# Two matmul layers behind a linear recurrence: full 128-row passes for the last 64 features, and another engine for the scaling of the weights

## The chip, the cores and the metric

One core of a Trainium2 chip runs the whole program. The metric is the device time of one execution in microseconds (us); lower is better. The engines named below are TensorE (PE; its weight loads are listed apart as PEld), VectorE (DVE), ScalarE (ACT), GpSimd (POOL) and SyncE (SP), whose queue issues the DMAs.

## What is computed

The reference has three stages. The first is a recurrence over 768 steps for 4 x 8 heads of 40 features; its output is laid out as 3072 tokens of 320 features. The other two are layers with 2048 hidden units each:

```
x = attention(r, k, v, w, a, b)          # (3072, 320), float32
h = x @ w_in;   x = (h * cos(h)) @ w_out
h = x @ w_in2;  x = (s * relu(h)**2 + b) @ w_out2
```

The weights come as 64-bit floats. The answer has to be near that of float32, and the kernel reaches it with pairs of 16-bit numbers: a value is kept as a high half (rounded to 16 bits) and a low half (what the rounding left out), and a product is made of high x high, high x low and low x high.

## The kernel before, in words

The tokens are cut into 12 chunks of 256 (4 batches x 64 steps). For each chunk the program runs the recurrence (`prep`, `chain`), then layer one (`m1_*`), then layer two (`m2_*`). A layer's 2048 hidden units are 16 blocks `ff` of 128, taken in 8 pairs `p`. For one block TensorE makes the hidden values `hp` (128 hidden units by 256 tokens, `first`), ScalarE, VectorE and GpSimd turn them into two 16-bit halves `gh` and `gl` (`m1_g`, `m2_g`), and TensorE makes the output sums `op` out of these (`m1_s`, `m2_s`).

**The product with 320 features.** The contraction over 320 features is cut into 128 + 128 + 64 rows. The first two parts take three passes each: high weights x high input, high x low, low x high. The 64-row rest is packed. Its tile of weights has 128 rows: one half of the rows holds the high weights, the other half the low ones (`rows` says which half; it changes with every pair `p`), and the inputs are there twice, in the rows 0 to 63 and 64 to 127. One pass over all 128 rows with the high inputs gives high x high and low x high together. What is left is high weights x low inputs over 64 rows alone: this is the tail. `tail` issues it as a matmul with 64 rows, and `tails` brings two of them side by side, that of the last block of the pair before and that of the first block of this pair, since these lie in different halves of the rows. So a block has seven passes of 128 rows and a tail of 64 rows, each with 256 columns. A tail clears the accumulation of its `hp` tile (`start`) for the first block of a pair, and `hp` of pair p is complete only when `tails` of pair p + 1 has run; so `mlp` calls `m1_g` or `m2_g` of pair p behind the first block of pair p + 1.

**The weights.** Each block of weights is loaded as 64-bit words; three VectorE instructions turn these into float32 in place (`float32`). Then `w_in_chunk` and `w_out_chunk` make the halves: ScalarE writes the high half (times 1024), GpSimd multiplies the float32 block by 1024 in place, and GpSimd subtracts the high half from it, which gives the low half. For `w_in` the subtraction is two instructions: one over 128 rows and 256 columns, and one over the 64 rows of the packed part. For half of the blocks of the second layer's `w_out` (`k % 4 < 2`, 8 of 16) one VectorE instruction multiplies and subtracts, and GpSimd has nothing to do. The first layer's weights are made during the first chunk of the recurrence; those of the second layer are made when the buffers of the recurrence come free, near the end of it (12 blocks into the freed space, then 4 more).

**What sets the order.** The program is first recorded, instruction by instruction (`Recorder.add`), and a planner (`Recorder.schedule`) with its own costs for each instruction then gives every engine its order; `emit` (line 406) issues it, so that almost every row of the profile has line 406, and the tiles' names tell the rows apart. Work of layer one is so placed between the short matmuls of the recurrence. An engine runs its own list strictly in that order.

**Names.** `hp` are the hidden sums, `op` and `opx` the output sums, `xs` and `x2s` the inputs of layer one and two; `w`, `w2b`, `wraw` are blocks of `w_in`, `v`, `v2b`, `vraw` blocks of `w_out`; `kb`, `kbh`, `kbl` and `ar`, `arh`, `arl` are inputs of the recurrence with their halves, `XX` its decays, `yhl` its result. The lines of the text are: `w_in_chunk` 578, `w_out_chunk` 590, `tail` 1043, `tails` 1048, `first` 1055, `mlp` 1236.

Of the kernel before, what the change touches and what calls it, by code (L numbers as in the profile page):

```python
# [10 lines left out]
F32 = mybir.dt.float32  # L11
# [4 lines left out]
AF = mybir.ActivationFunctionType  # L16
ALU = mybir.AluOpType
# [9 lines left out]
NC = S // C  # L27
NFF = FF // 128
TB = B * C
# [3 lines left out]
SW = 1024.0  # L33
# [412 lines left out]
class Fast:  # L446
# [131 lines left out]
    def w_in_chunk(self, dst, name, k):  # L578
        nc = self.nc
        st = self.float32(self.RAW["i", dst.tensor.name, k])  # L580
        m = self.wtags[3] // 128
        wv = dst[:, k * m:k * m + m].rearrange("p f a n -> p a f n")
        sv = st.rearrange("p a (f n) -> p a f n", f=m)
        nc.scalar.activation(wv[:, 0:3], sv, AF.Copy, scale=SW)
        nc.gpsimd.tensor_scalar(out=st, in0=st, scalar1=SW, scalar2=1.0, op0=ALU.mult, op1=ALU.mult)
        nc.gpsimd.tensor_tensor(out=wv[:, 3:5], in0=sv[:, 0:2], in1=wv[:, 0:2], op=ALU.subtract)
        r = slice(64 - self.rows(k * m), 128 - self.rows(k * m))
        nc.gpsimd.tensor_tensor(out=wv[r, 2], in0=sv[r, 2], in1=wv[r, 2], op=ALU.subtract)

    def w_out_chunk(self, dst, name, k):  # L590
        nc = self.nc
        st = self.float32(self.RAW["o", dst.tensor.name, k])
        nc.scalar.activation(dst[:, k, 0], st, AF.Copy, scale=SW)
        if name == "v2" and k % 4 < 2:
            nc.vector.scalar_tensor_tensor(out=dst[:, k, 1], in0=st, scalar=SW, in1=dst[:, k, 0], op0=ALU.mult, op1=ALU.subtract)
            return
        nc.gpsimd.tensor_scalar(out=st, in0=st, scalar1=SW, scalar2=1.0, op0=ALU.mult, op1=ALU.mult)
        nc.gpsimd.tensor_tensor(out=dst[:, k, 1], in0=st, in1=dst[:, k, 0], op=ALU.subtract)

    def w_in_test(self, parts, name, k):  # L600
# [439 lines left out]
        for h in range(2):  # L1040
            self.nc.sync.dma_start(out=x[h * 64:h * 64 + 64, :, 2], in_=v[:, 256:320].rearrange("f p n -> p f n"))

    def tail(self, ps, w, x, ff):

        r = slice(self.rows(ff), self.rows(ff) + 64)
        self.nc.tensor.matmul(ps[:, ff % 2], w[ff][r, 2], x[r, 2, 1], start=(ff % 2 == 0), stop=True, skip_group_check=True)

    def tails(self, p, w, x):
        hp = self.HP
        hp[p] = self.ph.tile([128, 2, TB], F32, tag="at", bufs=8, name="hp")  # L1050
        if p:
            self.tail(hp[p - 1], w, x, 2 * p - 1)
        self.tail(hp[p], w, x, 2 * p)

    def first(self, p, k, w, x):
        ff, hp = 2 * p + k, self.HP
        for a, i, b in ((0, 0, 0), (0, 0, 1), (1, 1, 0), (1, 1, 1), (2, 2, 0), (3, 0, 0), (4, 1, 0)):
            self.nc.tensor.matmul(hp[p][:, k], w[ff][:, a], x[:, i, b], start=False, stop=True, skip_group_check=True)
        if ff == NFF - 1:
            self.tail(hp[p], w, x, ff)  # L1060


    def m1_t(self, c, p):
        x = self.XS[c]
        self.tails(p, self.W1, x.rearrange("p f i k t -> p i k f t"))

    def m1_f(self, c, p, k):
        x = self.XS[c]
# [32 lines left out]
    def x2(self, j):  # L1101
# [7 lines left out]
        for m in range(2):  # L1109
# [4 lines left out]
                for b in range(2):  # L1114
                    nc.tensor.transpose(ps[:, i, b], q[:, b, m, i * 128:i * 128 + 128], self.ident)
            nc.vector.tensor_copy(xs[:, :, :, m], ps)

    def m2_t(self, j, p):
        x = self.XS[NC + j]
        self.tails(p, self.W2, x.rearrange("p i b m t -> p i b (m t)"))  # L1120

    def m2_f(self, j, p, k):
        x = self.XS[NC + j]
# [109 lines left out]
                  (self.yt, c, pg), (self.ts, c, pg)]:  # L1233
            self.do(*f)

    def mlp(self, t, f, g, s, j, lo=0, hi=NFF // 2 + 2):
        lag = 2
        for p in range(lo, hi):
            for k in range(2):
                if p < NFF // 2:  # L1240
                    if k == 0:
                        self.do(t, j, p)
                    self.do(f, j, p, k)
                if k == 0 and 1 <= p <= NFF // 2:
                    self.do(g, j, p - 1)
                if p >= lag:
                    self.do(s, j, p - lag, k)
        if s == self.m1_s:
            self.nc.base[self.nc.blk] = (NC - 1 - j) * 22

    def run(self, es0):
        tc, nc = self.tc, self.nc
        for n in ("AN BT A0 UF M1 DT RAW HL UN UD X XV V TT G IN KB AR Z ND U RP R SS SD SHL XT M2 XS HP GH OP Y").split():
            setattr(self, n, {})
        with ExitStack() as es:
            pc = es0.enter_context(tc.tile_pool(name="const", bufs=1))
            dr = es.enter_context(tc.tile_pool(name="dram", bufs=1, space=DRAM))
            self.x0 = dr.tile([NC, 2, H, D, 4 * C], F16, name="x0")
            self.x1 = dr.tile([NC, 2, 128, DM], F32, name="x1")
            self.consts(pc)  # L1260
            rec = self.nc = Recorder(nc, {"any": {"at", "xs", "q"}, "cls": {"XT": 3, "rhp": 3, "hp": 3, "op": 2, "xs": 2, "M2": 2, "q": 4, "att": 6}})
            rec.sink.add(self.junk.tensor.name)
            pool = lambda s, n, **k: rec.pool(s.enter_context(tc.tile_pool(name=n, bufs=1, **k)), n)
            self.pm = pool(es, "mlp")
            self.ph = self.po = self.pp = pool(es, "psum", space=PSUM)
            pw = pool(es, "wt")
            self.w1 = pw.tile([128, NFF, 5, 128], F16, name="w1")
            self.v1 = pw.tile([128, NFF, 2, DM], F16, name="v1")
            es_p, es_a = ExitStack(), ExitStack()
            self.pst = pool(es_p, "prep", side="right")  # L1270
            self.pa = pool(es_a, "attn")
            self.XX = self.pa.tile([128, 4, 32, 33], F32, name="XX")
            self.ST = {pg: self.pa.tile([128, 8, 40], F32, name=f"ST{pg}") for pg in range(2)}
            self.YT = self.pst.tile([128, 16, 32], F32, name="YT")
            rec.vector.tensor_copy(self.YT[:, :, 16:32], bc(self.up[:, 0:16], 1, [128, 16, 16]))
            self.wtags = self.pm, "xs", 5, 128
            self.ff0 = 0
            self.W1, self.V1 = ([t[:, f] for f in range(NFF)] for t in (self.w1, self.v1))
            m1 = self.m1_t, self.m1_f, self.m1_g, self.m1_s
            m2 = self.m2_t, self.m2_f, self.m2_g, self.m2_s  # L1280
            self.prep(0)
            for c in range(NC):
                if c + 1 < NC:
                    self.prep(c + 1)
                if c == 0:
                    self.weights("w1", "v1", self.w1, self.v1)
                self.chain(c, 0)
                self.chain(c, 1)
                self.do(self.xs, c)
                self.do(self.x1_load, c)  # L1290
                if c < NC - 1:
                    self.mlp(*m1, c)
                else:
                    self.nc.base[self.nc.blk] = 26
                if c == 3:
                    self.tests("w1", "v1", (self.w1,), (self.v1,), 250)
            rec.schedule(until=("prep",))
            es_p.close()
            es_v = ExitStack()
            pv = pool(es_v, "late_v", side="right")  # L1300
            n = 12
            v2 = pv.tile([128, n, 2, DM], F16, name="v2")
            w2 = pv.tile([128, n, 5, 128], F16, name="w2")
            self.second(w2, v2, 0)
            self.W2, self.V2 = ([t[:, f] for f in range(n)] for t in (w2, v2))
            self.do(self.x2, 0)
            self.mlp(*m2, 0, 0, n // 2)
            half = dict(self.HP), dict(self.GH)
            self.mlp(*m1, NC - 1)
            self.HP, self.GH = half  # L1310
            rec.schedule(until=("attn",))
            es_a.close()
            es_b = ExitStack()
            self.pb = pool(es_b, "late")
            v2b = self.pb.tile([128, NFF - n, 2, DM], F16, name="v2b")
            w2b = self.pb.tile([128, NFF - n, 5, 128], F16, name="w2b")
            self.wtags = self.pb, "braw", 8, 128
            self.second(w2b, v2b, n)
            self.W2 += [w2b[:, f] for f in range(NFF - n)]
            self.V2 += [v2b[:, f] for f in range(NFF - n)]  # L1320
            for j in range(NC):
                if j:
                    self.do(self.x2, j)
                self.mlp(*m2, j, 0 if j else n // 2)
                if j == 3:
                    self.tests("w2", "v2", (w2, w2b), (v2, v2b), 750)
            rec.schedule()
            es_b.close()
            es_v.close()
            self.nc = nc  # L1330
            return self.verdict(pc)
# [156 lines left out]
```

## Time and profile before

| | |
|---|---|
| median of 3 runs | 1153.78 us (1151.23 to 1154.51) |
| the profiled execution | 1145.39 us, of which 1143.7 us from its first to its last instruction |
| PE busy | 1005.5 us (88%) |
| DVE busy | 739.4 us (65%) |
| ACT busy | 717.4 us (63%) |
| POOL busy | 444.0 us (39%) |
| mean granted TensorE clock | 0.959 |

The profiled execution is one run. Busy time counts each moment once, and matmuls overlap, so a PE that is busy throughout can still have passes that are dearer than others: what one costs is read from the distance between starts. The share of an engine over the whole run says little here, because the run has four stretches that differ: the first weights and the first chunk of the recurrence, the recurrence mixed with layer one, the second weights, and layer two alone. The table of windows below keeps them apart.

### The profile page before, as it was taken

What the parts mean: (1) busy time and instruction counts of PE and PEld (TensorE: products, weight loads), DVE (VectorE), ACT (ScalarE), POOL (GpSimd) and SP (SyncE); (2) the same over time, 40 slices, a digit from 0 to 9 for tenths busy, and PEclk for the clock granted to TensorE, in tenths of its full rate; (3) what the DMA queues carried; (4) which work ended last, traced back from release to release, by engine and by line L of the source; (5) the groups of instructions that cost most, each with busy time, mean ns of one, the idle gap of its engine ahead of it and who ended that gap; (6) DMA issues with size and microseconds to landing.
All of it is one profiled execution on the core that took longest, in us unless ns stands there. A gap on an engine that the chain in (4) does not pass through costs nothing.

```text
span 1143.7 us, 37859 instructions
## 1 busy us (share of the span) xinstructions
PE 1005.5 (88%) x16094; PEld 768.7 (67%) x16094; DVE 739.4 (65%) x1414; ACT 717.4 (63%) x1544; POOL 444.0 (39%) x454
## 2 busy tenths in 40 slices
PE   3037698998999999898999998599999999999996
PEld 3036586776777777676777776377777777777774
DVE  6999986658666649575668469992444544444443
ACT  3356596787878788695888667463556554444442
POOL 2696756346454635554557135872100000000000
PEclk9998689899989999999999999699999999999999
DMA  9563535254535334535353244610111111111000
GB/s 278 203 210 131 193 99 175 78 164 140 165 107 160 114 117 140 163 104 163 113 165 128 89 166 153 203 39 14 31 26 27 26 26 26 26 25 27 12 15 20
DMA packets 90664, 121.88 MB, mean 107 GB/s; under 512 B 17624, under 2 KB 66136, under 8 KB 89464
## 3 DMA queue, kind: packets, MB, share of 16 engines
q1 hardware_dynamic: 90488, 119.39, 32.9%
q8 instruction: 128, 2.10, 0.8%
q14 instruction: 48, 0.39, 0.1%
HBM read 74.58 MB, written 11.80 MB: 76 GB/s over the span
## 4 chain that ended last, share of the span: by engine, by line
PE 70%; DVE 8%; DMA 7%; ACT 5%; POOL 4%; issue 3%; SPq 2%; POOLq 0%; ACTq 0%; DVEq 0%
PE hp L406 26%; PE op L406 25%; PE rhp L406 4%; SPq L406 2%; PE ytp L406 2%; PE uhp L406 2%; DVE XX L406 2%; DMA XX<-in_w 2%; DVE v L406 2%; PE txp L406 1%; PE s1p L406 1%; PE spp L406 1%; PE dtp L406 1%; PE opx L406 1%; DMA XT<-XT 1%
## 5 line engine op out<-in xcount | busy, mean ns | idle before, releaser
L406 PEld LDWEIGHTS <-w 128*128 128x128 f16 (+1 forms) x2688 | 240.3, 98 | 86.3 <-issue 34.8
L406 PE MATMUL op<-v,gh 128*128 128x320 f16 x1296 | 274.8, 302 | 0.4 <-ACT gh L406 0.4
L406 PE MATMUL hp<-xs,w 128*128 128x256 f16 (+1 forms) x1536 | 205.5, 279 | 14.3 <-DMA xs<-x 7.4
L406 PE MATMUL op<-v,gl 128*128 128x320 f16 x648 | 195.0, 301 | 1.1 <-POOL gl L406 1.1
L406 POOL TENSOR_TENSOR gl<-q,gh 128x512 f16<-128x512 f32 x96 | 116.4, 1216 | 194.9 <-ACT gh L406 185.6
L406 PEld LDWEIGHTS <-gh 128*128 128x128 f16 x1536 | 135.7, 98 | 57.2 <-issue 3.7
L406 PE MATMUL hp<-x2s,w 128*128 128x256 f16 (+1 forms) x1152 | 149.6, 274 | 0.0
L406 DVE SCALAR_TENSOR_TENSOR q<-q,s_t 128x512 f32<-128x512 f32 x96 | 73.0, 760 | 102.4 <-ACT q L406 101.3
L406 ACT ACTIVATE q<-hp 128x512 f32<-128x512 f32 x96 | 57.0, 594 | 103.1 <-PE hp L406 103.1
L406 DVE SCALAR_TENSOR_TENSOR gl<-q,b_t,gh 128x512 f16<-128x512 f32 x96 | 72.2, 752 | 68.7 <-ACT gh L406 63.9
L406 DVE SCALAR_TENSOR_TENSOR q<-hp,q 128x512 f32<-128x512 f32 x96 | 65.8, 685 | 72.4 <-ACT q L406 71.4
L406 ACT ACTIVATE gh<-q,b_t 128x512 f16<-128x512 f32 x96 | 69.1, 720 | 60.7 <-DVE q L406 60.5
L406 PEld LDWEIGHTS <-gl 128*128 128x128 f16 x768 | 75.5, 98 | 31.8 <-POOL gl L406 1.9
L406 ACT ACTIVATE q<-hp,half_pi 128x512 f32<-128x512 f32 x96 | 65.3, 681 | 29.7 <-PE hp L406 29.0
L406 POOL TENSOR_TENSOR kb<-kb,XX 128x512 f32<-128x512 f32 x44 | 57.6, 1320 | 46.4 <-DVE XX L406 42.5
L406 ACT ACTIVATE gh<-q 128x512 f16<-128x512 f32 x96 | 59.9, 626 | 23.4 <-DVE q L406 22.4
L406 DVE TENSOR_TENSOR_SCAN XX<-XX,starts 128x264 f32<-128x264 f32 x96 | 68.6, 768 | 7.9 <-DMA XX<-in_w 4.6
L406 PEld LDWEIGHTS <-KB 120*128 120x128 f16 (+1 forms) x704 | 28.9, 101 | 53.6 <-DMA KB<-kbl 34.4
L406 PE MATMUL rhp<-UF,M 64*64 64x40 f32 (+1 forms) x1536 | 52.4, 226 | 7.8 <-ACT UF L406 7.4
L406 POOL TENSOR_TENSOR arl<-ar,arh 128x1024 f16<-128x1024 f32 x22 | 48.0, 2182 | 28.6 <-ACT arh L406 28.4
L406 POOL TENSOR_TENSOR kbl<-kb,kbh 128x1024 f16<-128x1024 f32 x22 | 47.8, 2173 | 28.6 <-ACT kbh L406 27.4
L406 ACT ACTIVATE XT<-txp 80x1024 f16<-80x1024 f16 (+1 forms) x52 | 48.0, 948 | 11.6 <-PE txp L406 11.2
(194 smaller groups left out, 1925.1 us busy)
## 6 DMA issues: line engine op xcount, KB each, us to landing
XX<-in_w SPq DMA_DIRECT2D x12, 1056.0 KB
kb<-in_kb SPq DMA_DIRECT2D x24, 512.0 KB
ar<-in_ar SPq DMA_DIRECT2D x22, 512.0 KB
w<-in_w SPq DMA_DIRECT2D x20, 384.0 KB
v<-in_v SPq DMA_DIRECT2D x22, 320.0 KB
KB<-kbh SPq DMA_DIRECT2D x88, 80.0 KB
ars<-arh SPq DMA_DIRECT2D x88, 80.0 KB
wraw<-in_w SPq DMA_DIRECT2D x12, 384.0 KB
```

The lines of the kernel that those rows point to most:

```text
L406: f(*a, **k)
```

## The change

`first` makes eight passes of 128 rows for every block. The tail becomes the pass (2, 2, 1): the whole packed tile of weights, high and low, times the low inputs. Beside high x low this adds low x low, which the kernel before left out. `tail`, `tails`, `m1_t` and `m2_t` are gone; `first` allocates the `hp` tile at the first block of a pair, and `mlp` calls `m1_g` or `m2_g` of pair p right behind its second block.

In `w_in_chunk` and `w_out_chunk` the scaling in place is an instruction of ScalarE, for all 64 blocks (16 in each of w1, v1, w2 and v2). GpSimd loses 56 scalings, and it makes all the low halves: the 8 VectorE instructions for `v2` are gone, and 8 subtractions of GpSimd are there in their place.

```diff
@@ w_in_chunk
         nc.scalar.activation(wv[:, 0:3], sv, AF.Copy, scale=SW)
-        nc.gpsimd.tensor_scalar(out=st, in0=st, scalar1=SW, scalar2=1.0, op0=ALU.mult, op1=ALU.mult)
+        nc.scalar.activation(st, st, AF.Copy, scale=SW)
         nc.gpsimd.tensor_tensor(out=wv[:, 3:5], in0=sv[:, 0:2], in1=wv[:, 0:2], op=ALU.subtract)
@@ w_out_chunk
         nc.scalar.activation(dst[:, k, 0], st, AF.Copy, scale=SW)
-        if name == "v2" and k % 4 < 2:
-            nc.vector.scalar_tensor_tensor(out=dst[:, k, 1], in0=st, scalar=SW, in1=dst[:, k, 0], op0=ALU.mult, op1=ALU.subtract)
-            return
-        nc.gpsimd.tensor_scalar(out=st, in0=st, scalar1=SW, scalar2=1.0, op0=ALU.mult, op1=ALU.mult)
+        nc.scalar.activation(st, st, AF.Copy, scale=SW)
         nc.gpsimd.tensor_tensor(out=dst[:, k, 1], in0=st, in1=dst[:, k, 0], op=ALU.subtract)
@@ tail, tails, first
-    def tail(self, ps, w, x, ff):
-
-        r = slice(self.rows(ff), self.rows(ff) + 64)
-        self.nc.tensor.matmul(ps[:, ff % 2], w[ff][r, 2], x[r, 2, 1], start=(ff % 2 == 0), stop=True, skip_group_check=True)
...
     def first(self, p, k, w, x):
-        ff, hp = 2 * p + k, self.HP
-        for a, i, b in ((0, 0, 0), (0, 0, 1), (1, 1, 0), (1, 1, 1), (2, 2, 0), (3, 0, 0), (4, 1, 0)):
-            self.nc.tensor.matmul(hp[p][:, k], w[ff][:, a], x[:, i, b], start=False, stop=True, skip_group_check=True)
-        if ff == NFF - 1:
-            self.tail(hp[p], w, x, ff)
+        ff = 2 * p + k
+        if k == 0:
+            self.HP[p] = self.ph.tile([128, 2, TB], F32, tag="at", bufs=8, name="hp")
+        for n, (a, i, b) in enumerate(((0, 0, 0), (0, 0, 1), (1, 1, 0), (1, 1, 1), (2, 2, 0), (2, 2, 1), (3, 0, 0), (4, 1, 0))):
+            self.nc.tensor.matmul(self.HP[p][:, k], w[ff][:, a], x[:, i, b], start=(ff % 2 == 0 and n == 0), stop=True, skip_group_check=True)
@@ mlp
-    def mlp(self, t, f, g, s, j, lo=0, hi=NFF // 2 + 2):
+    def mlp(self, f, g, s, j, lo=0, hi=NFF // 2 + 2):
...
             for k in range(2):
                 if p < NFF // 2:
-                    if k == 0:
-                        self.do(t, j, p)
                     self.do(f, j, p, k)
-                if k == 0 and 1 <= p <= NFF // 2:
-                    self.do(g, j, p - 1)
+                    if k == 1:
+                        self.do(g, j, p)
```

The number of matmuls is the same in both: a tail of 64 rows goes, a pass of 128 rows comes. The planner orders everything anew. Three places show how.

TensorE in the middle of layer two, before. The rows are weight loads and matmuls in turn. The first two matmuls here are the last full passes of one block; the two behind them are a pair of tails, one into the old `hp` tile (14331), one into the new one (14337):

```order
 L406 LDWEIGHTS w2_13086
 L406 MATMUL hp_14327<-x2s_14323,w2_13086 128x256
 L406 LDWEIGHTS w2_13086
 L406 MATMUL hp_14327<-x2s_14323,w2_13086 128x256
 L406 LDWEIGHTS w2_13086
 L406 MATMUL hp_14331<-x2s_14323,w2_13086 128x256
 L406 LDWEIGHTS w2_13086
 L406 MATMUL hp_14337<-x2s_14323,w2_13086 128x256
```

The same place now:

```order
 L406 LDWEIGHTS w2_13090
 L406 MATMUL hp_14345<-x2s_14328,w2_13090 128x256
 L406 LDWEIGHTS w2_13090
 L406 MATMUL hp_14345<-x2s_14328,w2_13090 128x256
 L406 LDWEIGHTS w2_13090
 L406 MATMUL hp_14339<-x2s_14328,w2_13090 128x256
 L406 LDWEIGHTS w2_13090
 L406 MATMUL hp_14339<-x2s_14328,w2_13090 128x256
```

A block's eight passes now stand together, all in one `hp` tile, and the next block follows with its own eight; there are no matmuls of 64 rows between them.

GpSimd in the first stretch, before. `kbl` and `arl` are low halves that the recurrence waits for, and `v` and `w` are weights of layer one; TENSOR_SCALAR on `v` or `w` is the scaling, TENSOR_TENSOR the subtraction:

```order
 L406 TENSOR_SCALAR v_136<-v_136 128x320
 L406 TENSOR_TENSOR v_136<-v_136 128x320
 L406 TENSOR_TENSOR kbl<-kb,kbh 128x1024
 L406 TENSOR_TENSOR ar<-ar,XX 128x8x64
 L406 TENSOR_SCALAR v_136<-v_136 128x320
 L406 TENSOR_SCALAR ar<-ar 128x8x64
 L406 TENSOR_SCALAR v_136<-v_136 128x320
 L406 TENSOR_TENSOR v_136<-v_136 128x320 x2
 L406 TENSOR_TENSOR arl<-ar,arh 128x1024
 L406 TENSOR_SCALAR w_135<-w_135 128x384
 L406 TENSOR_SCALAR v_136<-v_136 128x320
```

The same place now:

```order
 L406 TENSOR_TENSOR v_136<-v_136 128x320
 L406 TENSOR_TENSOR kbl<-kb,kbh 128x1024
 L406 TENSOR_TENSOR ar<-ar,XX 128x8x64
 L406 TENSOR_TENSOR v_136<-v_136 128x320
 L406 TENSOR_SCALAR ar<-ar 128x8x64
 L406 TENSOR_TENSOR v_136<-v_136 128x320
 L406 TENSOR_TENSOR w_135<-w_135 128x256
 L406 TENSOR_TENSOR arl<-ar,arh 128x1024
 L406 TENSOR_TENSOR w_135<-w_135 64x128
```

The order of `kbl`, `ar` and `arl` among each other is the same; the scalings of `v` and `w` between them are gone, and the subtractions have moved a place or two.

ScalarE later in the first stretch, before: `wraw` is a block of `w_in` in a buffer of its own, `SHL`, `R`, `arh` and `YT` belong to the recurrence:

```order
 L406 ACTIVATE w_135<-wraw 128x384
 L406 ACTIVATE XT<-txp 40x512
 L406 ACTIVATE w_135<-w_135 128x384
 L406 ACTIVATE SHL<-ST_145 128x8x40
 L406 ACTIVATE w_135<-wraw 128x384
 L406 ACTIVATE R<-rhp 32x320 x2
 L406 ACTIVATE arh<-ar 128x1024
```

The same place now:

```order
 L406 ACTIVATE w_135<-wraw 128x384
 L406 ACTIVATE wraw<-wraw 128x384
 L406 ACTIVATE SHL<-ST_145 128x8x40
 L406 ACTIVATE w_135<-wraw 128x384
 L406 ACTIVATE wraw<-wraw 128x384
 L406 ACTIVATE v_136<-v_136 128x320 x2
 L406 ACTIVATE arh<-ar 128x1024
```

Behind each high half (`w<-wraw`) stands the scaling in place (`wraw<-wraw`), and instructions of the recurrence such as `SHL` and `arh` now have these ahead of them on ScalarE.

## Rows read from the trace of the kernel before

**Rows 1.** Windows: time, each engine's busy us (instructions), granted clock, DMA share, GB/s.

```profile
core 0: us, PE busy (x) PEld busy (x) DVE busy (x) ACT busy (x) POOL busy (x), PEclk, DMA share, GB/s
0.00:150.00 150.00, 70.44 (x1498) 59.68 (x1499) 137.76 (x254) 76.11 (x178) 96.16 (x137) 0.87 0.61 196
150.00:690.00 540.00, 507.52 (x10853) 394.30 (x10853) 355.54 (x787) 417.95 (x923) 280.13 (x219) 0.97 0.42 135
690.00:741.00 51.00, 34.07 (x526) 24.91 (x524) 48.66 (x87) 29.02 (x60) 34.65 (x44) 0.80 0.54 173
741.00:1134.00 393.00, 392.99 (x3219) 289.71 (x3219) 195.22 (x279) 193.10 (x380) 33.03 (x56) 1.00 0.10 26
```

**Rows 2.** Timeline of PE in layer two: start, busy, instructions merged.

```profile
903.38 1.15 PE L406 MATMUL hp<-x2s,w 128*128 128x256 f16 x9
904.45 0.45 PE L406 MATMUL op<-v,gh 128*128 128x320 f16 x2
...
905.28 0.93 PE L406 MATMUL hp<-x2s,w 128*128 128x256 f16 x7
906.04 0.43 PE L406 MATMUL op<-v,gh 128*128 128x320 f16 x2
```

**Rows 3.** Timeline of the weight loads (PEld) at the same place.

```profile
903.24 0.78 PEld L406 LDWEIGHTS <-w 128*128 128x128 f16 x7
...
904.23 0.10 PEld L406 LDWEIGHTS <-w 64*128 64x128 f16 x2 [0.21 <-issue]
```

**Rows 4.** Chain that ended last, layer two: start, us, what; one chunk to the next.

```profile
898.98 2.93 PE hp L406 x24
...
927.59 2.93 PE hp L406 x24
```

**Rows 5.** PE groups by shape, 741 to 1134: count, busy us, mean ns, idle before.

```profile
L406 PE MATMUL hp<-x2s,w 64*128 64x256 f16 x144 | 23.6, 279 | 0.0
...
L406 PE MATMUL hp<-x2s,w2b 64*128 64x256 f16 x48 | 10.1, 279 | 0.0
```

**Rows 6.** PE groups by shape, 150 to 690.

```profile
L406 PE MATMUL hp<-xs,w 64*128 64x256 f16 x155 | 27.1, 280 | 5.0 <-ACT SD L406 1.4 <-DVE q L406 1.2 <-ACT q L406 1.2
```

**Rows 7.** DVE, tiles v and w, 0 to 150: ns min/median/max, first and last start.

```profile
L406 DVE SCALAR_TENSOR_TENSOR v<-v x26: 466/858/2353, 36.1 to 136.5; 128x320 int32<-128x320 int32 x26
...
L406 DVE SCALAR_TENSOR_TENSOR w<-w x24: 545/894/2478, 20.5 to 117.2; 128x384 int32<-128x384 int32 x24
```

**Rows 8.** POOL groups by shape, 0 to 150.

```profile
L406 POOL TENSOR_SCALAR v<-v 128x320 f32<-128x320 f32 x13 | 7.6, 587 | 2.2 <-ACT v L406 1.3
L406 POOL TENSOR_SCALAR w<-w 128x384 f32<-128x384 f32 x12 | 7.4, 619 | 22.4 <-ACT w L406 17.0 <-issue 2.3 <-DMA v<-in_v 2.1
```

**Rows 9.** Chain that ended last, first stretch.

```profile
67.34 0.48 POOL v L406
...
69.02 2.35 POOL kbl L406
...
71.86 3.13 DMA KB<-kbh
```

**Rows 10.** ACT groups by shape, 0 to 150.

```profile
L406 ACT ACTIVATE w<-w 128x384 f16<-128x384 f32 x12 | 6.5, 553 | 9.5 <-DVE w L406 9.4
L406 ACT ACTIVATE v<-v 128x320 f16<-128x320 f32 x13 | 6.3, 488 | 9.7 <-DVE v L406 7.2 <-POOL v L406 2.4
```

**Rows 11.** POOL and DVE groups by shape, 690 to 760.

```profile
L406 POOL TENSOR_SCALAR wraw<-wraw 128x384 f32<-128x384 f32 x8 | 5.1, 643 | 3.7 <-ACT w2b L406 3.2
...
L406 POOL TENSOR_TENSOR v<-v 128x320 f16<-128x320 f32 x4 | 3.6, 919 | 0.2
...
L406 POOL TENSOR_SCALAR w<-w 128x384 f32<-128x384 f32 x4 | 3.3, 822 | 9.2 <-ACT w L406 6.4 <-issue 2.8
...
L406 POOL TENSOR_SCALAR v<-v 128x320 f32<-128x320 f32 x4 | 3.0, 750 | 1.3 <-ACT v L406 0.7 <-POOL w L406 0.4
...
L406 DVE SCALAR_TENSOR_TENSOR v<-v 128x320 f16<-128x320 f32 x5 | 3.8, 767 | 0.0
```

More of the change, by code (lines that the diff above doesn't have):

```diff
@@ L1041, in x1_load @@
             self.nc.sync.dma_start(out=x[h * 64:h * 64 + 64, :, 2], in_=v[:, 256:320].rearrange("f p n -> p f n"))
-    def tail(self, ps, w, x, ff):
-        r = slice(self.rows(ff), self.rows(ff) + 64)
-        self.nc.tensor.matmul(ps[:, ff % 2], w[ff][r, 2], x[r, 2, 1], start=(ff % 2 == 0), stop=True, skip_group_check=True)
[L1048 to L1053, printed above, removed]
-    def first(self, p, k, w, x):
-        ff, hp = 2 * p + k, self.HP
-        for a, i, b in ((0, 0, 0), (0, 0, 1), (1, 1, 0), (1, 1, 1), (2, 2, 0), (3, 0, 0), (4, 1, 0)):
-            self.nc.tensor.matmul(hp[p][:, k], w[ff][:, a], x[:, i, b], start=False, stop=True, skip_group_check=True)
-        if ff == NFF - 1:
-            self.tail(hp[p], w, x, ff)
-    def m1_t(self, c, p):
-        x = self.XS[c]
-        self.tails(p, self.W1, x.rearrange("p f i k t -> p i k f t"))
+    def first(self, p, k, w, x):
+        ff = 2 * p + k
[3 more added lines that the diff above has]
+            self.nc.tensor.matmul(self.HP[p][:, k], w[ff][:, a], x[:, i, b], start=(ff % 2 == 0 and n == 0), stop=True, skip_group_check=True)
     def m1_f(self, c, p, k):
@@ L1116, in x2 @@
             nc.vector.tensor_copy(xs[:, :, :, m], ps)
-    def m2_t(self, j, p):
-        x = self.XS[NC + j]
-        self.tails(p, self.W2, x.rearrange("p i b m t -> p i b (m t)"))
     def m2_f(self, j, p, k):
@@ L1278, in run @@
             self.W1, self.V1 = ([t[:, f] for f in range(NFF)] for t in (self.w1, self.v1))
-            m1 = self.m1_t, self.m1_f, self.m1_g, self.m1_s
-            m2 = self.m2_t, self.m2_f, self.m2_g, self.m2_s
+            m1 = self.m1_f, self.m1_g, self.m1_s
+            m2 = self.m2_f, self.m2_g, self.m2_s
             self.prep(0)
```

## The prediction

> **What bounds the kernel now.** I read the windows first, because the run falls into four stretches, then the chain of waits to see which engine each stretch hangs on, then the groups by shape for prices, and the timeline where a price could not be had from a mean.
>
> The windows [rows 1] show it at a glance. From 741 to 1134 us (layer two and the last chunk of layer one) PE is busy 392.99 of 393.00 us at the full granted clock, 1.00 (2.4 GHz); nothing else is above half. A nanosecond saved on PE there is a nanosecond off the run. From 150 to 690 (recurrence mixed with layer one) PE is busy 507.5 of 540 us: mostly PE too, with waits of the recurrence between. From 0 to 150 it is VectorE: 137.8 of 150 us, with PE at 70. From 690 to 741 (second weights) it is VectorE again, 48.7 of 51 us, while PE has 34 and its granted clock falls to a mean of 0.80. So the change touches two bounds: PE's passes in the two long stretches, and the traffic of VectorE and GpSimd in the two stretches where weights are converted.
>
> **Part 1: the tails.** A mean duration will not do here, since matmuls overlap: a 64-row pass has a mean of 279 ns [rows 5] and a full pass one like it. What counts is the distance between starts. In the timeline of layer two [rows 2] seven `hp` matmuls begin at 905.28 and the next group at 906.04: 0.76 us, or 0.109 us for a full pass. A little earlier nine `hp` matmuls take from 903.38 to 904.45: 1.07 us. The weight loads [rows 3] say what these nine were: seven loads of 128 rows, then two of 64 rows, and before these two a gap of 0.21 us that nothing explains ("issue"). So the pair of tails took 1.07 - 0.76 = 0.31 us. Two full passes in its place take 2 x 0.109 = 0.22 us. The change, which on paper spends twice the rows, saves 0.093 us for each pair.
>
> There are eight pairs in a chunk. One chunk of layer two takes from 898.98 to 927.59 in the chain [rows 4], 28.61 us, and should take 27.87 us. The stretch from 741 on holds 393 / 28.61 = 13.7 such chunks, 110 pairs, 10.2 us. The groups by shape agree as to the count: 144 + 48 = 192 passes of 64 rows in layer two alone [rows 5], which is 12 chunks x 16. All of it lies on the path: **10 us**.
>
> Here a rule of the Trainium skill speaks against the change. TensorEngine Tiling (Array Packing), section Theoretical Speedup, gives up to 2x for a contraction of 64 rows or fewer, because two row tiles work at the same time; by that alone the pairs cost what one full pass costs and the change would lose. The same page, section Key Properties, says that a change of the tiling mode drains the engine; the gap of 0.21 us in [rows 3] is what such a drain would look like, and the measured pair is dearer than two passes.
>
> From 150 to 690 there are 155 passes of 64 rows [rows 6], some 77 pairs. If each saved the same, that is 7.2 us. But there many pairs stand beside short matmuls of the recurrence, which use fewer rows as well, so that a switch is paid anyway, and PE waits for other things in 32 of the 540 us. Between 0 and 7.2 I take **5 us**, nearer the upper end since PE is busy in 94% of the stretch.
>
> `hp` of a pair is complete one block earlier, and ScalarE's `q` can start earlier. In the last stretch PE never waits, so that is worth nothing there; in the mixed stretch it is room for the planner that I do not price.
>
> **Part 2: scaling on ScalarE.** In the first 150 us GpSimd loses 13 scalings of `v` at 587 ns and 12 of `w` at 619 ns [rows 8], 15.0 us of its 96 [rows 1]. It matters in two ways. One is GpSimd's queue: in the chain a scaling of 0.48 us and its subtraction stand ahead of `kbl` (2.35 us), behind which a DMA of 3.13 us has to land before PE goes on [rows 9]. The other is VectorE, the bound of this stretch. The same conversion of `v` takes 466 ns at best and 2353 ns at worst, that of `w` 545 to 2478 [rows 7]; the long ones have the size of GpSimd's `kbl`. VectorE and GpSimd hinder each other, so each GpSimd instruction less may give VectorE time back. From above the gain is all 15.0 us. From below: the 25 instructions go to ScalarE, at 553 and 488 ns for the same shapes [rows 10], 13 us in all. ScalarE is busy 76 of 150 us, but it also copies what the recurrence waits for, and if every one of these stood in the way it would cost those 13 us. Most of VectorE's excess must come from the GpSimd instructions that stay (81 of 96 us), so I stay near zero and on the good side: **3 us**.
>
> The Trainium skill, SBUF — State Buffer, section SBUF: two separate sides, says that VectorE and GpSimd share a pair of ports by an exclusive lock held for a whole instruction, and that ScalarE never waits for anyone. [Rows 7] agree with the first; no row here shows the second.
>
> **Part 3: the second weights.** Between 690 and 760 GpSimd loses 8 scalings at 643 ns, 4 at 822 and 4 at 750 [rows 11], 11.4 us. It gains the subtractions that VectorE made before: VectorE loses 5 instructions at 767 ns, 3.8 us, and GpSimd makes 5 at 919 ns [rows 11], 4.6 us. Best case for VectorE, if each GpSimd instruction delays it in full: 11.4 - 4.6 + 3.8 = 10.6 us. Worst: the 16 added ScalarE instructions, about 0.5 us each [rows 10], stand ahead of `q` and `gh` for layer one: 8 us lost. `gl` of layer one queues on GpSimd behind the subtractions, so GpSimd's net relief is 6.8 us and not 11.4. VectorE is the bound and certainly loses 3.8 us of its own; I take **3 us**. The other three blocks whose subtraction moves are converted beside saturated PE and cost nothing as long as it stays so.
>
> **The sum.** 10 + 5 + 3 + 3 = 21 us. The profiled execution took 1145.39 us (1143.7 of span), so it would take 1124. The three runs have a median of 1153.78, 8.4 us above the profiled one; I take the same 21 us off it: **1133 us**.
>
> **Rivals.**
> - **Only the matmuls gain.** The weight stretches trade GpSimd's queue for ScalarE's and end where they did: 1153.8 - 15 = 1139, or 1144 if the mixed stretch gives nothing either. For it: ScalarE sits between VectorE and GpSimd for every block. Against it: it is about half idle in both stretches [rows 1].
> - **VectorE is freed in full.** Parts 2 and 3 give 15 and 10.6 us in place of 6: 1133 - 20 = 1113. For it: VectorE is above 90% busy in both stretches. Against it: other GpSimd work would fill the places.
> - **Tails really ran at half price.** If a pair of tails costs no more than one full pass, because both run at once, the change adds 0.109 us for each of 192 pairs in the two layers: 21 us, 1175. It decides if the gap in [rows 3] is work hidden elsewhere. Against it stands the start of the next group in [rows 2], which is later by that gap. (This is the rule of the Trainium skill, TensorEngine Tiling (Array Packing), Theoretical Speedup, told above.)
> - **ScalarE becomes the wait (slower).** Place: the first 150 us and 690 to 741, where ScalarE's list is strict and copies for the recurrence now stand behind scalings. Price: 13 us there and 8 us here, and parts 2 and 3 give nothing, so +21; against the matmuls' 15 that is 1160. It decides once these scalings fill ScalarE's idle time ahead of a copy that PE waits for; with 74 of 150 us idle that is far off on average, not in every place.
> - **Nothing to see.** The planner orders everything anew and loses by worse places what the passes gain: 1154. The saturated stretch leaves little room for that.
>
> **How the numbers follow.** A measurement of this kernel tells about 0.3% from no change, 3.5 us. Forecast 0.52 (own range 1124 to 1138); only the matmuls 0.22; VectorE freed in full 0.15; nothing 0.03; tails at half price 0.03; ScalarE the wait 0.05. Faster: 0.52 + 0.22 + 0.15 = 0.89; same 0.03; slower 0.08. The range reaches up to 1145, just past the matmuls alone, and down to 1114, where parts 2 and 3 give nearly all they can.
>
> **What would show it.** Right, if no load of 64 rows for `w` is left; if layer two repeats every 27.9 us with PE full at clock 1.00; if the conversions of `v` and `w` on VectorE have a lower median in the first 150 us; and if PE's full stretch starts a few us before 741. Wrong, if the distance of a full pass rises above 0.109 us; if the chain in the first stretch shows ScalarE with weights where it had GpSimd; or if 150 to 690 does not get shorter though PE has less to do.

## The result and the profile after

The change takes 1135.36 us (median of 4 runs, 1131.19 to 1140.77) against 1152.87 for the kernel before in the same job (1151.23 to 1154.51). The ratio is 0.9845, with a 95% interval of 0.9805 to 0.9884: 17.5 us faster. A second measurement beside the experiments gave 0.9842 (0.9815 to 0.987). The forecast was 1133. Medians here are of all runs; the ratios leave out runs more than 1.5% above the fastest of the same kernel, which are one run of E6 and two of E8.

The two profiled executions differ by less, 1145.39 and 1140.77 us: the one of before lies below all runs that make its median, the one of after is the slowest of its four. So what follows reads the traces for what single places cost, and the medians for the totals.

The windows of after, with the same columns and stretches as [rows 1]:

```profile
core 0: us, PE busy (x) PEld busy (x) DVE busy (x) ACT busy (x) POOL busy (x), PEclk, DMA share, GB/s
0.00:150.00 150.00, 72.27 (x1471) 60.59 (x1471) 133.16 (x259) 92.22 (x210) 81.25 (x110) 0.85 0.62 196
150.00:690.00 540.00, 501.14 (x10674) 402.31 (x10673) 341.82 (x782) 411.74 (x911) 269.03 (x207) 0.95 0.42 135
690.00:741.00 51.00, 36.06 (x683) 27.66 (x682) 35.02 (x71) 39.30 (x87) 31.39 (x36) 0.86 0.43 131
741.00:1134.00 393.00, 387.26 (x3272) 314.50 (x3270) 197.82 (x297) 201.88 (x401) 32.35 (x55) 1.00 0.12 33
```

In the first stretch GpSimd went from 96.2 to 81.3 us and ScalarE from 76.1 to 92.2, as the change says. VectorE fell from 137.8 to 133.2. Yet the first pass of layer one starts no earlier here, at 151.6 us where it was 150.8 (in E0, the same kernel, at 148.6). In the third VectorE fell from 48.7 to 35.0 of 51 us: it is the bound there no longer. PE is not full at once from 741 on (387 of 393 us).

The chain of waits of after in layer two (start, us, what), for [rows 4]:

```profile
898.88 2.62 PE hp L406 x24
...
926.56 2.62 PE hp L406 x24
```

One chunk is 926.56 - 898.88 = 27.68 us, where it was 28.61. The same 24 `hp` passes take 2.62 us in place of 2.93. The timeline of PE at that place, for [rows 2]:

```profile
900.46 1.04 PE L406 MATMUL hp<-x2s,w 128*128 128x256 f16 x8
901.34 0.43 PE L406 MATMUL op<-v,gh 128*128 128x320 f16 x2
```

Eight passes of a block start at 900.46 and the next group at 901.34: 0.88 us, or 0.11 us each, the price of before. The weight loads of the block, for [rows 3]:

```profile
900.36 0.86 PEld L406 LDWEIGHTS <-w 128*128 128x128 f16 x8
901.23 0.21 PEld L406 LDWEIGHTS <-gh 128*128 128x128 f16 x2
```

No load of 64 rows for `w` is left, and no gap of 0.21 us ("issue") at this place.

VectorE's conversions in the first 150 us (ns min/median/max, first and last start), for [rows 7]:

```profile
L406 DVE SCALAR_TENSOR_TENSOR v<-v x26: 477/618/2405, 34.8 to 128.7; 128x320 int32<-128x320 int32 x26
...
L406 DVE SCALAR_TENSOR_TENSOR w<-w x24: 527/628/2376, 20.7 to 110.0; 128x384 int32<-128x384 int32 x24
```

The medians fell from 858 to 618 and from 894 to 628 ns; the best and the worst are within 5% of what they were.

### The profile page after: what moved, and what is told of

It is laid out like the page before. It is cut to its first block, busy times and chain, and to the rows that moved or that the text cites. A ratio compares the mean times of both kernels' runs of the same rounds, so it can differ in the third digit from the quotient of the medians.

```text
span 1139.1 us, 37990 instructions
## 1 busy us (share of the span) xinstructions
PE 996.7 (88%) x16094; PEld 805.1 (71%) x16094; DVE 707.8 (62%) x1406; ACT 745.1 (65%) x1608; POOL 414.0 (36%) x406
## 5 line engine op out<-in xcount | busy, mean ns | idle before, releaser
L406 PEld LDWEIGHTS <-w 128*128 128x128 f16 x2688 | 260.5, 100 | 57.6 <-issue 9.1
L406 PE MATMUL hp<-xs,w 128*128 128x256 f16 x1536 | 202.8, 284 | 14.8 <-DMA xs<-x 7.6
L406 PEld LDWEIGHTS <-gh 128*128 128x128 f16 x1536 | 144.3, 98 | 49.9 <-issue 3.2
L406 PE MATMUL hp<-x2s,w 128*128 128x256 f16 x1152 | 141.8, 273 | 0.0
L406 DVE SCALAR_TENSOR_TENSOR q<-hp,q 128x512 f32<-128x512 f32 x96 | 65.4, 684 | 77.6 <-ACT q L406 76.1
L406 ACT ACTIVATE R<-rhp 32x320 f32<-32x320 f32 x96 | 41.1, 429 | 25.6 <-PE rhp L406 23.8
L406 PE MATMUL uhp<-R,DT 32*32 32x40 f32 x1536 | 41.1, 205 | 16.1 <-ACT DT L406 7.0
```

The lines of the kernel that those rows point to most:

```text
L406: f(*a, **k)
```

## The experiments

The change has three parts that can act: the passes, the scaling, and the planner's new order, which comes with each of the others. The experiments change them one at a time. "Old order" means that every engine runs the order of the kernel before; "own order" that the planner made a new one. E3, E5, E6 and E10 issue the tails over 128 rows and so add low x low, as the change does. The diffs show the lines that matter; where the planner is told another cost, the lines that hand it over are left out in part.

**E0: the change again**, for a measurement beside the others; no edit.

> The change as it is, timed again beside the others. My theory: about 17 us less than the kernel before, with a chunk of layer two at 27.7 us (28.61 before). Rival (run-to-run scatter made most of the 17 us): under 10 us less.

1135.35 us against 1154.15, ratio 0.9842 (0.9815 to 0.987). E0 to E3 ran in one job with the same runs of before.

**E1: the passes alone, own order.** The change in `first` and `mlp`, with the weights as before:

```diff
-        for a, i, b in ((0, 0, 0), (0, 0, 1), (1, 1, 0), (1, 1, 1), (2, 2, 0), (3, 0, 0), (4, 1, 0)):
+        for n, (a, i, b) in enumerate(((0, 0, 0), (0, 0, 1), (1, 1, 0), (1, 1, 1), (2, 2, 0), (2, 2, 1), (3, 0, 0), (4, 1, 0))):
```

> The eight full passes and the earlier call of m1_g and m2_g alone; the scaling stays on GpSimd, and VectorE keeps its 8 instructions for v2. My theory: 15 us less (10 in layer two alone, 5 in the mixed stretch), 27.7 us for a chunk of layer two. Rival (the weight stretches bring the gain of the mixed stretch): 10 us less, all of it in layer two.

1150.94 us, ratio 0.9975 (0.9951 to 1.0): hardly faster than before, although its layer two has the change's chunk of 27.68 us. What the passes gave there was lost elsewhere.

**E2: the scaling alone, own order.** The change in `w_in_chunk` and `w_out_chunk`, with the tails as before:

```diff
-        nc.gpsimd.tensor_scalar(out=st, in0=st, scalar1=SW, scalar2=1.0, op0=ALU.mult, op1=ALU.mult)
+        nc.scalar.activation(st, st, AF.Copy, scale=SW)
```

> The scaling on ScalarE and all low halves on GpSimd alone; the tails of 64 rows stay. My theory: 6 us less, with PE full from about 735 instead of 741, and a chunk of layer two still at 28.6 us. Rival (ScalarE takes the place of GpSimd in the waits): within 3 us of the kernel before.

1146.16 us, ratio 0.9928 (0.9903 to 0.9953), a little more than was expected; but PE is not full from 735 on, it still waits at 770 us for `x2q`. E1 and E2 together give 3.2 + 8.0 = 11.2 us, the change 18.8: with a new order each time, the medians of the parts do not add up.

**E3: full tails on the old order.** The tails stay where they are, over 128 rows in place of 64; the planner is told the cost of 64 rows, so no instruction moves on any engine:

```diff
-        self.nc.tensor.matmul(ps[:, ff % 2], w[ff][r, 2], x[r, 2, 1], start=(ff % 2 == 0), stop=True, skip_group_check=True)
+        self.nc.half = [w[ff][r, 2], x[r, 2, 1]]
+        self.nc.tensor.matmul(ps[:, ff % 2], w[ff][:, 2], x[:, 2, 1], start=(ff % 2 == 0), stop=True, skip_group_check=True)
+        self.nc.half = None
```

> The kernel before with every tail issued over all 128 rows, at its old place: the planner is given the old cost and the old rows, so each engine's order is the same, row by row, as before. My theory (a change between 64 and 128 rows is what a pair of tails pays for): a chunk of layer two falls from 28.61 to 27.9 us, 10 us less in layer two and up to 7 in the mixed stretch, so 10 to 17 us less in all. Rival (the new order of the passes is what saves time): 28.6 us or more for a chunk and no gain. Rival (two 64-row passes cost one full pass): 8 passes more for a chunk, 29.5 us, and 21 us lost.

1134.69 us, ratio 0.9843 (0.9816 to 0.9869): 19.5 us by the medians, as much as the whole change. The chain of E3 in layer two:

```profile
923.38 2.62 PE hp L406 x24
...
951.06 2.62 PE hp L406 x24
```

Again 27.68 us, with twice the rows in every tail and nothing else different. So the gain of layer two is the price of the 64-row passes, and neither the earlier `m2_g` nor the order. E1 has as many full passes, in the same job, and is 16.3 us slower, with intervals well apart: the same passes in another order (and with each block's eighth pass among its own) lose nearly all that they give. The loss is in the mixed stretch: the recurrence's last store (`x<-yhl`) starts at 742.3 us in the trace of E1 and at 727.7 in that of E3.

**E4: the kernel before, two more profiled runs**; no edit.

> The kernel before once more, for its trace. Theory (its first profiled execution was a lucky one in the stretch from 150 to 741, granted clock 0.959 against 0.945 to 0.950 in all the others): about 1153 us, layer two as before (28.61 us for a chunk), and the start of PE's full stretch 5 to 10 us later than 741. Rival (the profile makes this kernel faster): about 1145 us again.

> As the run ahead of it: the kernel before a third time, so that its mixed stretch has a scatter. Theory: 1150 to 1156 us and a mean granted clock of 0.95. Rival: 1145 us and 0.959.

1149.23 and 1151.18 us (11 other runs of before in this job: 1147.33 to 1159.93, median 1153.93). The 17 runs of before beside E0 to E3 have mean granted clocks of 0.944 to 0.954, so the first profile, with 0.959, stands above all of them. The cores view of the profiled run of before and of the two of E4 (span, mean granted TensorE clock):

```profile
core 0: 1143.7 us, clock 0.959
```

```profile
core 0: 1147.5 us, clock 0.954
```

```profile
core 0: 1149.5 us, clock 0.950
```

One program, one order, 5.8 us apart, with the longer span at the lower clock. The last `hp` pass of layer one starts at 802.5, 806.4 and 808.8 us in these three, and from there to the end it is 341.2, 341.1 and 340.7: the scatter lies ahead of that, and not in layer two.

**E6: full tails, own order.** As E3, but the planner is told the true cost:

```diff
-        self.nc.tensor.matmul(ps[:, ff % 2], w[ff][r, 2], x[r, 2, 1], start=(ff % 2 == 0), stop=True, skip_group_check=True)
+        self.nc.tensor.matmul(ps[:, ff % 2], w[ff][:, 2], x[:, 2, 1], start=(ff % 2 == 0), stop=True, skip_group_check=True)
```

> The kernel before with every tail issued over 128 rows, as in the run with the old plan, but with the planner told so: it counts the pass at its full cost and orders everything anew. Theory (a new order in the mixed stretch moves the time by several us either way, whatever the edit): layer two as with the old plan (27.7 us for a chunk), but the total differs from 1135 us by 5 us or more, with the difference standing at the start of PE's full stretch. Rival (the order is of little weight, and what made the passes alone slow was the earlier call of m1_g): 1135 us within 3.

1143.84 us, ratio 0.9886 (0.9838 to 0.9935): slower than E3 by 9 us in the medians and by 5 in the ratios, though the two differ in the order alone. The intervals overlap, so this is likely and not shown. The mixed stretch of E3:

```profile
150.00:690.00 540.00, 505.32 (x10859) 405.26 (x10855) 354.48 (x786) 416.75 (x923) 279.34 (x217) 0.96 0.42 135
```

and of E6:

```profile
150.00:690.00 540.00, 506.56 (x10666) 403.65 (x10665) 334.13 (x776) 409.70 (x906) 268.13 (x203) 0.94 0.41 130
```

PE is equally busy, but E6 gets 193 matmuls fewer done, at a granted clock of 0.94 in place of 0.96. A part of that lies ahead of the window, since the first pass of layer one starts at 157.2 us in E6 and at 151.2 in E3; and this execution of E6 (1149.26 us) lies above its median.

**E8: the passes alone, at the old cost.** E1, with the pass (2, 2, 1) counted by the planner as a tail was:

```diff
-        c = self.cost(eng, method, outs[0], aps, k)
+        c = (256, 16, 0.5, 128) if self.half else self.cost(eng, method, outs[0], aps, k)
```

> The eight passes together and the earlier m1_g and m2_g, scaling on GpSimd, as in the run with the passes alone, but the planner counts the pass (2, 2, 1) at the old cost of a tail. Theory (the planner's dearer pass is what made both plans with it slow, 1151 and 1144 us): about 1135 us. Rival (the passes together, with hp complete earlier, lead to the slow plan): 1145 us or more. Rival (a plan is a draw, and neither is the cause): anything between 1130 and 1152.

1150.39 us, ratio 0.9962 (0.993 to 0.9994), like E1. So the planner's figure for the pass is not what makes E1 slow. In E8, as in E6, the first pass of layer one already starts late, at 156.9 us (E3: 151.2). Over their 12 runs each E1 and E8 have a median of the mean granted clock of 0.938 and 0.936; before has 0.949 in both jobs, E3 0.950. The clock is lower in these orders by about as much, 1.3%, as the 16 us are of the time. What in an order brings the lower clock was not found, nor whether the clock is the cause or follows from PE's waits.

**E7: a lone pass of 64 rows.** The change, order and all, with the pass (2, 2, 1) over 64 rows; low x low is left out, as before:

```diff
-            self.nc.tensor.matmul(self.HP[p][:, k], w[ff][:, a], x[:, i, b], start=(ff % 2 == 0 and n == 0), stop=True, skip_group_check=True)
+            r = slice(self.rows(ff), self.rows(ff) + 64) if n == 5 else slice(0, 128)
+            self.nc.tensor.matmul(self.HP[p][:, k], w[ff][r, a], x[r, i, b], start=(ff % 2 == 0 and n == 0), stop=True, skip_group_check=True)
```

> The change with each engine's order as it is, only that the pass (2, 2, 1) goes over 64 rows again, alone between passes of 128 rows (low x low is left out, as before). Theory (what is paid is the switch between 64 and 128 rows, there and back, about 0.2 us above a full pass when a 64-row pass stands alone): 16 x 0.2 = 3.2 us more for a chunk of layer two, 30.9 in place of 27.7 us, and 40 to 75 us more in all than the change. Rival (a 64-row pass is slow only as one of a pair): 27.7 us. Rival (fewer rows are cheaper): below 27.7.

1204.11 us, ratio 1.0445 (1.0393 to 1.0496), 69 us above the change. Its chain in layer two:

```profile
965.38 3.25 PE hp L406 x24
...
996.42 3.25 PE hp L406 x24
```

A chunk is 31.04 us, 3.36 above 27.68, and it has 16 such passes: 0.21 us each, on top of what a full pass costs. The weight loads of E7 show where:

```profile
1001.00 0.56 PEld L406 LDWEIGHTS <-w2b 128*128 128x128 f16 x5
1001.77 0.33 PEld L406 LDWEIGHTS <-w2b 64*128 64x128 f16 x3 [0.21 <-issue]
1002.11 0.54 PEld L406 LDWEIGHTS <-w 128*128 128x128 f16 x5
1002.86 0.87 PEld L406 LDWEIGHTS <-w 64*128 64x128 f16 x8 [0.21 <-issue]
```

Every turn from 128 rows to 64 has the gap of 0.21 us ahead of it. (Groups of loads are merged under the form of the first one, so "x3" is the load of 64 rows and the two full ones that follow it.) A pair side by side, as before, pays it once for two.

The kernel before has both cases in its own trace, a lone tail at 899.99 and the pair of [rows 3] at 904.23. The weight loads, each with the next load behind it:

```profile
899.99 0.09 PEld L406 LDWEIGHTS <-w2b 64*128 64x128 f16 x1 [0.21 <-issue]
900.21 0.66 PEld L406 LDWEIGHTS <-w 128*128 128x128 f16 x7
...
904.23 0.10 PEld L406 LDWEIGHTS <-w 64*128 64x128 f16 x2 [0.21 <-issue]
904.45 0.11 PEld L406 LDWEIGHTS <-gh 128*128 128x128 f16 x2
```

Gap and distance to the next load are the same, 0.21 and 0.22 us, for one tail and for two; both loads of the pair lie within 0.10 us. So the two tails of a pair do run at the same time and cost what one costs. What makes them dear is the turn, which is paid for either.

**E9: the scaling alone, old order.** The 56 scalings of GpSimd are issued on ScalarE at the places in the program that they had, and nothing else moves; the 8 VectorE instructions for `v2` stay:

```diff
-        nc.gpsimd.tensor_scalar(out=st, in0=st, scalar1=SW, scalar2=1.0, op0=ALU.mult, op1=ALU.mult)
+        nc.add("gpsimd", "tensor_scalar", lambda out, in0: nc.real.scalar.activation(out, in0, AF.Copy, scale=SW), (), {"out": st, "in0": st})
```

> The kernel before with its 56 scalings issued on ScalarE instead of GpSimd, each at the place in the program's order where GpSimd's stood; the planner is not told, so all else keeps its order, row by row, and VectorE keeps its 8 instructions for v2. Theory (fewer GpSimd instructions give VectorE time back): 5 to 8 us less, as the scaling with a plan of its own gave 8, and the conversions of v and w on VectorE in the first 150 us get shorter. Rival (the 8 us were the new plan's): within 3 us of the kernel before. Rival (ScalarE's copies for the recurrence wait behind the scalings): slower.

1144.66 us against 1152.77, ratio 0.9918 (0.9889 to 0.9948): 8.1 us by the medians. The conversions of the second run of E4:

```profile
L406 DVE SCALAR_TENSOR_TENSOR v<-v x26: 470/780/2354, 36.1 to 137.0; 128x320 int32<-128x320 int32 x26
...
L406 DVE SCALAR_TENSOR_TENSOR w<-w x24: 546/896/2479, 20.6 to 117.3; 128x384 int32<-128x384 int32 x24
```

and of E9:

```profile
L406 DVE SCALAR_TENSOR_TENSOR v<-v x26: 476/742/2352, 35.3 to 131.2; 128x320 int32<-128x320 int32 x26
...
L406 DVE SCALAR_TENSOR_TENSOR w<-w x24: 546/620/2484, 20.6 to 114.1; 128x384 int32<-128x384 int32 x24
```

The same instructions in the same order have lower medians, above all `w` (896 to 620 ns), and the last `v` starts 5.8 us earlier. (The medians scatter: E10, with the same order, has 645 for `v` and 706 for `w`. And an order alone lowers them too: E1, with the scaling on GpSimd, has 738 and 730.) GpSimd's own list is shorter as well: the `kbl` that the chain of before has at 69.02 [rows 9] stands in that of E9 at

```profile
66.38 2.49 POOL kbl L406
```

So both ways that the prediction named show, VectorE's time and GpSimd's list, and E9 does not tell their shares apart. The first pass of layer one starts at 145.5 us, where it was 150.8 in the profiled run of before and 150.2 and 150.3 in E4. ScalarE's longer list costs little: it shows in that chain of E9 with a scaling of 0.54 us at 60.39.

**E5: the scaling of the change and full tails, own order.** E2 with the tails at their old places over 128 rows, at the old cost; the edits are those of E2 and E3, except that the planner is told of 128 rows for the inputs of a tail. Its order is neither that of E2 nor the old one.

> The scaling on ScalarE as in the change, with the tails kept at their places but issued over 128 rows, and with the planner's old cost for them. Theory (the two gains add, 8 us for the scaling and 19 for the rows): 1127 us. Rival (both draw on the same waits of the mixed stretch, so that they don't add): 1134 us, as each of the two good kernels.

1130.68 us, ratio 0.9818 (0.9779 to 0.9857). This new order costs little if anything: by the medians it is 4 us behind E10 below, which has the old one, and the intervals overlap.

**E10: both parts, old order.** E3 and E9 in one kernel; the diff is that of both.

> Both parts with the old order: tails over 128 rows and the scalings on ScalarE, on the plan of the kernel before. Theory (the two gains add): the 19 us of the rows and what the run ahead of it shows for the scaling, 1127 to 1130 us. Rival (they draw on the same waits): 1135 us as with the rows alone.

1126.35 us, ratio 0.9789 (0.974 to 0.9837): 26.4 us, close to E3 and E9 together, 19.5 + 8.1 = 27.6. On the old order the parts add up. It is the fastest of all, below the change by 9 us in the medians and by 6 in the ratios; the two were not run side by side, and their intervals overlap (0.9815 to 0.987 for the change).

Where the change falls behind E10: its first `hp` pass of layer one starts at 148.6 us (in E0) in place of 145.4, and the last one at 805.3 in place of 794.7. So the loss lies ahead of that. PE has a long wait for `xs` at the second weights, and behind it E0 is 7.1 us late. PE's next group in E0 and in E10:

```profile
733.88 9.44 PE L406 MATMUL hp<-xs,w 128*128 128x256 f16 x68 [7.99 <-DMA xs<-x]
```

```profile
726.78 8.33 PE L406 MATMUL hp<-xs,w 128*128 128x256 f16 x49 [6.87 <-DMA xs<-x]
```

SP's queue of E0 ahead of that:

```profile
724.07 0.75 SPq L406 DMA_DIRECT2D x<-yhl  x2
729.01 0.62 SPq L406 DMA_DIRECT2D wraw<-in_w  x1
729.68 1.29 SPq L406 DMA_DIRECT2D xs<-x  x2
...
734.10 0.59 SPq L406 DMA_DIRECT2D wraw<-in_w  x1
...
735.38 1.00 SPq L406 DMA_DIRECT2D wraw<-in_w  x1
...
738.55 0.57 SPq L406 DMA_DIRECT2D wraw<-in_w  x1
```

and of E10:

```profile
720.38 0.74 SPq L406 DMA_DIRECT2D x<-yhl  x2
...
722.32 1.60 SPq L406 DMA_DIRECT2D xs<-x  x2
724.14 0.57 SPq L406 DMA_DIRECT2D wraw<-in_w  x1
...
725.43 0.57 SPq L406 DMA_DIRECT2D wraw<-in_w  x1
...
727.17 0.55 SPq L406 DMA_DIRECT2D wraw<-in_w  x1
...
728.53 0.60 SPq L406 DMA_DIRECT2D wraw<-in_w  x1
```

The recurrence's last store (`x<-yhl`) comes 3.7 us later in E0, and the load of weights behind it waits until it has landed, which the chain of E0 has as

```profile
724.41 4.45 DMA x<-yhl
```

In E10 the two loads of `xs` that PE waits for stand ahead of this load of weights, in E0 behind it, where they start 7.4 us later. So the planner's new order for SP's queue holds PE up for 3 to 4 us here. VectorE loses time at the same place. The window of E0:

```profile
690.00:741.00 51.00, 34.47 (x571) 26.80 (x571) 34.03 (x72) 36.50 (x82) 27.78 (x34) 0.83 0.48 151
```

and of E10:

```profile
690.00:741.00 51.00, 36.38 (x536) 28.50 (x535) 46.95 (x86) 35.69 (x77) 28.13 (x34) 0.80 0.60 192
```

VectorE has 17 us of idle time in E0. Its waits from 690 to 760 (us in total, times, longest) in E0:

```profile
DVE wraw L406 <- DMA xs<-x: 7.7, 1, 7.7
DVE w L406 <- DMA w<-in_w: 3.8, 3, 2.3
```

The last four blocks of weights are asked for 5 to 10 us later than in E10, and VectorE, freed of its `v2` work, stands and waits for them. All this is read from two traces; a kernel with only these loads moved was not tried.

## Why the prediction came out right

The time was right (1133 against 1135.36, inside the range and the forecast's own 1124 to 1138), and the mechanism of the largest term is shown. That the sum came so near is in part luck: the largest term was too small, the other three together left about half of their 11 us, and the new order, which took the rest, had no price. The figures below are read from medians and ratios, so each is good to a few us.

- **10 us in layer two: 12.7.** By the same count, 13.7 chunks, now with the measured 28.61 - 27.68 = 0.93 us. With 8 pairs in a chunk a pair saved 0.116 us, where the starts in [rows 2] gave 0.093. One reason is that a chunk has six pairs, one lone tail and one group of three, and a full pass in place of a lone tail saves about 0.2 us. E3 shows the cause with nothing moved.
- **5 us in the mixed stretch: 5 to 7 on the old order.** This is E3's gain less 12.7, with 18.1 us by its ratio or 19.5 by the medians; its interval (15.1 to 21.2 us) leaves 2.4 to 8.5, so the 5 was not refuted. E3's last pass of layer one starts at 802.4, that of E4 at 806.4 and 808.8; against the profiled run of before, at 802.5, nothing is seen.
- **3 + 3 us for the weights: about 8 on the old order** (6 to 13 by E9's interval), for the scalings alone. The 5 `v` instructions that left VectorE between 690 and 760 are not in E9; by themselves they were not measured. The exclusive lock that the Trainium skill states (SBUF — State Buffer, SBUF: two separate sides) agrees with 896 to 620 ns for `w` in E9, though how much of the 8 us comes of it is open.
- **Missing: the new order, 6 to 9 us lost.** The parts give 27.6 on the old order, and E10 26.4; the change gives 17.5 to 18.8. With 12.7 in layer two, 5 to 6 are left of the 11 that the other terms add up to. What the prediction lacked is in the sentence that calls the earlier `hp` "room for the planner that I do not price", and in the rival "nothing to see", which held that the saturated stretch leaves little room for a loss. The loss is not in that stretch but ahead of it: in the traces 3.2 us by the first pass of layer one (E0 against E10), and 3 to 4 at the second weights. That an order can cost much is clear from E1 against E3 (16 us); that this one cost 6 to 9 rests on E10 against the change, whose intervals overlap.
- **The rivals.** *Tails at half price* falls: E3 doubled the rows and became 19.5 us faster, where that rival asks for 21 slower. Its premise holds, though: the two tails of a pair run at once (E7 and the rows beside it). It falls because the gap of the turn is real and dearer than the half that is saved. The Trainium skill, TensorEngine Tiling (Array Packing), states both, up to 2x for 64 rows (Theoretical Speedup) and a drain at a change of mode (Key Properties). The traces agree with both: a pair costs what one tail costs, and the turn 0.21 us in E7. *ScalarE the wait* falls with E9 and E2. *Only the matmuls gain* falls on the old order, where the scaling is worth about 8 us (E9); in the change the new order took that back, and it is no faster than E3. *VectorE freed in full* would have given 1113; even E10 stays 13 above.
- **The signs.** No 64-row load, a chunk of 27.7 us at clock 1.00 and lower medians on VectorE are there, though the medians fall in E1 too and so say little of the scaling. "PE's full stretch starts a few us before 741" failed in the change: in E0 PE still waits at 755 us for `x2q`. In E10 it holds, with PE full from 730 on. Of the signs against, the distance of a full pass is unchanged. ScalarE with weights is on the chain of E0 in the first stretch, but only twice, at 59.64 and 60.21, for 0.55 us each. The third sign came true as far as the traces tell: from the first pass of layer one to the recurrence's last store E0 takes 575.8 us and after 579.3, where the three traces of before have 576.2 to 580.1, so the mixed stretch got no shorter beyond its scatter. (PE's 501 us of busy time from 150 to 690, in place of 507.5, say nothing, since fewer matmuls fell into that window.)

## What to carry to other kernels

Price a pass by the distance to the next start and look at what stands around it: a few passes over half the rows between full ones can cost more than the rows they save, even where two of them run at once, and a full pass that computes something superfluous may be cheaper. When an edit makes a planner order everything anew, measure the edit on the old order as well; the new order is a change of its own, and here one cost 16 of the 19 us that the edit gives (E1 and E3). And take an in-place helper off the engine that hinders the bound, even if the engine that gets it is busier.

## What was not expected of the hardware

- A turn from passes of 128 rows to 64 and back costs 0.21 us, about two full passes of 256 columns (0.109 us each), for one 64-row pass as for a pair in different halves of the rows, which runs at once. One lone 64-row pass per block cost 69 us over the run (E7).
- One program in one order scatters by more than 10 us (1146.95 to 1161.67 in 23 runs of before), with granted clocks from 0.943 to 0.956 in that job; the prediction had taken 0.3%, 3.5 us, for what a measurement can tell. In E8, E9, E10 and before the longer executions tend to have the lower clock. So two single profiles (4.6 us apart here) can say little of a change of 17.5.
- Two new orders (E1 and E8) had a lower mean clock in all their runs together, 0.938 and 0.936 at the median against 0.949, though the old order with the same passes kept 0.950. What in them lowers it stays open.
